# Scaling the top-k threshold on GpSimd in the main loop of an attention-and-FFN kernel, with a reordered tail

## The chip, the cores and the metric

The kernel runs on one core of a Trainium2 chip. The metric is the device time of one execution in microseconds (us). A core has a matmul engine (TensorE, PE in the profile; its weight loads are PEld), VectorE (DVE), ScalarE (ACT), GpSimd (POOL) and SyncE (SP, which here only starts DMAs). Each engine takes its instructions in the order in which the program wrote them and waits on semaphores for data of the others.

## The reference

Attention over 8 batches, 8 heads, 576 rows and a head size of 64, of which each row keeps only its 32 largest scores, and then a feed-forward layer with a squared ReLU:

```python
scores = scale * np.matmul(q, k.transpose(0, 1, 3, 2))
kth = np.partition(scores, -top_k, axis=-1)[..., -top_k:-top_k + 1]     # top_k = 32
mask = scores >= kth
scores = np.where(mask, scores, -1000000000.0)
scores = scores - np.max(scores, axis=-1, keepdims=True)
attn = np.exp(scores)
attn = attn / (np.sum(attn, axis=-1, keepdims=True) + 1e-09)
x = np.matmul(attn, v)                 # heads side by side: 4608 rows x 512
h = np.maximum(x @ w_in, 0.0)          # 512 x 2048
out = h * h @ w_out                    # 2048 x 512
```

## The kernel before

The rows of scores are worked off in 144 steps (U = 144). A step u holds two tiles of 128 rows by 576 scores. Lines 658 to 709 are the main loop over steps 0 to 124 (Z = U - 19 = 125); lines 721 to 762 are steps 125 to 141, and two steps and an ending are written out behind them. All work is issued in an order written out by hand: `pin` keeps every instruction at its place on its engine, so the order of the calls in a step is the order on each engine's queue.

What a step does for its two tiles:

- `scores(u + 2)` (L195): PE computes the scores of the step after next into the two halves sc_a and sc_b, and ACT copies each half to SBUF (L210), the two score copies of a step.
- `split(u + 1)` (L224): DVE folds the 576 scores of a row with maxima and minima into `cat` (L235, L236, L243, L244, and L242 where the far minimum is DVE's own). `small_mins(u + 1)` (L254) makes the remaining minima on POOL as an integer addition and subtraction (L258, L259). Where the planner has lent the far minimum to POOL, `far_copy(u + 1)` (L249) lets ACT copy the far maxima from PSUM (L252).
- `topk(u)` (L267): DVE finds the 32 largest in four rounds of eight (MAX8 at L277, MATCH_REPLACE8 at L281). In round 1 `negate` (L313) takes, in every second step and for two steps at once, the negated maximum on DVE (L318), and ACT adds a constant to it (`low`, L320), which is the bias of the exponentials.
- `cut(u - 1)` (L324): one small instruction on ACT multiplies the 32nd largest score of the step before by a huge negative constant (`edge`, L326). `below(u - 1, x)` (L328) is the mark: ACT computes a ReLU of scores times that constant plus `edge` into `kept` (L330), for each of the two tiles. `expo(u - 1, x)` (L336) is the exponential of a tile into `w_two` (L338). `mask(u - 1)` (L332) adds `kept` to `w_two` as integers on POOL (L334), and `turn(u - 1)` (L369) starts a DMA transpose on SP's queue into `wT`.
- `products(u - 3)` (L648): PE multiplies `wT` with the values (L399); column 64 is the sum of weights. `invert` or `invert_two` (L402, L407) is its reciprocal on DVE (L404, L411), and `place` (L420) scales and stores the output of a tile on ACT (L428, L436).
- The feed-forward layer is cut into pieces of some 1 to 2 us of matmuls, which `dense` and `piece` (L563, L554) put between the attention's matmuls. What an up piece leaves for ACT (a ReLU, L511) and POOL (the square, L514) is queued in `late` and issued by the next `flush`; so is the copy of a finished output (L538).
- `prepare` (L622) transposes and scales inputs of later heads (L135 to L149 on ACT, L155 on POOL, the values), with loads on SP's queue; 16 weight casts go to ACT or POOL (L600, L597). `verify` and `note` check now and then, on DVE and POOL (L303 to L311), that the shortcut of the top-k was exact.

`owe` and `pass_step` are a planner's account: each step books 4.6 us for ACT and 3.2 us for POOL besides what single jobs book, and 6.1 us are written off for each step; `split` lends to POOL, and a cast chooses its engine, by these accounts.

In the main loop a step's calls stand in this order: cut(u - 1) and the first mark; split(u + 1); place; far_copy(u + 1); second mark; round 0; checks; small_mins(u + 1); a dense piece; scores(u + 2); rounds 1 to 3; exponentials, mask and transpose of u - 1; flush; products(u - 3); a second dense piece; preparation. In the tail (`for u in range(Z, U - 2)`) the exponentials, mask and transpose of step u - 1 are issued in `weights(u - 1)`: for even u after small_mins, for odd u after round 3, since the constant of two steps is made together.

Of the kernel before, what the change touches and what calls it, by code (L numbers as in the profile page):

```python
# [13 lines left out]
f32 = mybir.dt.float32  # L14
# [3 lines left out]
ALU = mybir.AluOpType  # L18
AF = mybir.ActivationFunctionType
# [4 lines left out]
def kernel(  # L24
# [9 lines left out]
    nc = tc.nc  # L34
# [5 lines left out]
    scale = 1.0 / (D ** 0.5)  # L40
    STEEP = 2.0 ** 80
    PREV = 1.0 - 2.0 ** -24
    LOW, SPAN, FINE = -76.24618986, 11.0, 2.0 ** -60
# [3 lines left out]
    def pin(ins):  # L47
        tc.keep_in_program_order(ins)
        return ins
# [3 lines left out]
    def owe(**more):  # L53
        for e, t in more.items():
            debt[e] += t
# [10 lines left out]
    small = fast.enter_context(tc.tile_pool(name="small", bufs=2))  # L66
# [4 lines left out]
    fill = const.tile([128, 512], bf16, name="fill")  # L71
# [100 lines left out]
    for b in range(B):  # L172
# [8 lines left out]
        for c in range(4):  # L181
            steps += [((i, c, 0), (i, c, 1)) for i in range(p0 + 1, p0 + 4)]
            if c == 0:
                steps += rests(p0 + 2)
    U = len(steps)
    first = {}
    for u, two in enumerate(steps):
        for i, c, a in two:
# [3 lines left out]
    st = {}  # L192
# [31 lines left out]
    def split(u, meanwhile=None):  # L224
        d = st[u]
        lend = 2 < u < U - 20 and debt["G"] < 4.9 and debt["A"] < 5.4
        if lend:
# [35 lines left out]
    held_m = {}  # L263
# [3 lines left out]
    def topk(u, rounds=(0, 1, 2, 3), between=None):  # L267
        d = st[u]
        g = u % GROUP
        if g == 0 and 0 in rounds:  # L270
            held_m["m"] = small.tile([128, GROUP, 2, 4, 8], f32, name="m", bufs=2)
        m = d["m"] = [held_m["m"][:, g, :, r, :] for r in range(4)]
        cat = d["cat"]
        for r in rounds:
            at = WINDOWS[r]
            for x in range(2):
                pin(nc.vector.max(out=m[r][:, x, :], in_=cat[:, x, at]))  # L277
            if r == 3:
                break
            for x in range(2):  # L280
                pin(nc.vector.match_replace(out=cat[:, x, at], in_to_replace=m[r][:, x, :], in_values=cat[:, x, at], imm_value=NEG))  # L281
            if r == 1:
                negate(u)
            if r == 2 and between:
                between()
        if g == GROUP - 1 and 3 in rounds and u < U - 1:
            verify(u)
# [23 lines left out]
            pin(nc.gpsimd.tensor_tensor(odd, odd, wide[:, n], op=ALU.add))  # L311

    def negate(u):  # L313
        if u % 2 == 0:
            return
        g = u % GROUP
        neg = small.tile([128, 2, 2, 1], f32, name="neg", bufs=3)
        pin(nc.vector.tensor_reduce(neg[:, :, :, :], held_m["m"][:, g - 1:g + 1, :, 0:2, 0], axis=mybir.AxisListType.X, op=ALU.max, negate=True))  # L318
        low = small.tile([128, 2, 2, 1], f32, name="low", bufs=3)
        pin(nc.scalar.activation(low[:, :, :, :], neg[:, :, :, :], AF.Copy, bias=LOW))  # L320
        for n in range(2):
            st[u - 1 + n].update(neg=neg[:, n], low=low[:, n])

    def cut(u):  # L324
        edge = st[u]["edge"] = small.tile([128, 2, 1], f32, name="edge", bufs=3)
        pin(nc.scalar.activation(edge[:, :, :], st[u]["m"][3][:, :, 7:8], AF.Copy, scale=-STEEP * PREV))  # L326

    def below(u, x):  # L328
        d = st[u]
        pin(nc.scalar.activation(kept[u % 2][:, x, :].bitcast(f8)[:, 1:2 * S:2], d["s"][:, x, :], AF.Relu, bias=d["edge"][:, x, :], scale=STEEP, saturate=False))  # L330
# [5 lines left out]
    def expo(u, x):  # L336
        d = st[u]
        pin(nc.scalar.activation(w_two[u % 3][:, x, 0:S], d["s"][:, x, :], AF.Exp, bias=d["low"][:, x, :]))  # L338
# [6 lines left out]
    late, squares = [], []  # L345
    hold = {"squares": False, "out": False}

    def square():
        while squares:
            squares.pop(0)(nc.gpsimd)  # L350
# [7 lines left out]
    def expo_last(x):  # L358
        d = st[U - 1]
        e = kept[(U - 1) % 2][:, x, :].bitcast(bf16)  # L360
        pin(nc.scalar.activation(e, d["s"][:, x, :], AF.Exp, bias=d["neg"][:, x, :]))
        last_e.append(e)

    def mask_last(x):
        d = st[U - 1]
        pin(nc.vector.scalar_tensor_tensor(out=w_two[(U - 1) % 3][:, x, 0:S], in0=d["s"][:, x, :], scalar=d["m"][3][:, x, 7:8],
                                           in1=last_e[x], op0=ALU.is_ge, op1=ALU.mult))
# [80 lines left out]
    def x_unit(now, b, c):  # L448
# [21 lines left out]
        else:  # L470
            pin(nc.sync.dma_start_transpose(out=to, in_=x_tok[b, c][:, :]))
            ripe.setdefault(now + (3 if now < Z - 8 else 2), []).append(done)

    def rem_unit(now, b):
# [8 lines left out]
        if b % 2:  # L483
            rem = xt_rem[g % 2]
            stores = [[(slice(64 * a, 64 * a + 64), out[(b - 1 + a) * S + 512:(b + a) * S]) for a in range(2)]]
            go = lambda: block(lambda kh: rem[:, kh, :], stores)
            if now < Z - 1:
                ripe.setdefault(now + 1, []).append(go)
# [117 lines left out]
    load_pair(0)  # L606
    load_pair(1)
    busy = ps_one.tile([128, 512], f32, name="dn_ps")
    for n in range(11):
        pin(nc.tensor.matmul(out=busy[:, :], lhsT=fill[:, 0:128], rhs=fill[:, :], start=(n == 0), stop=(n == 10)))  # L610
    soon, coming = prep_units(0), 1
    for _ in range(4):
        soon.pop(0)()
# [26 lines left out]
    scores(1)  # L640


    Z = U - 19

    def ok(w):
        return 0 <= w < U

    def products(w):  # L648
        if ok(w):
            for x in range(2):  # L650
                weigh(w, x)
# [5 lines left out]

    for u in range(Z):
        f = u - 4
        pass_step()  # L660
        owe(A=4.6, G=3.2)
        if u > 0:
            cut(u - 1)
            below(u - 1, 0)
        if u == 0:
            topk(0, (0, 1))
            split(1)
            topk(0, (2, 3))
        else:
            split(u + 1, (lambda: invert_two(f)) if ok(f) and f % 2 else None)  # L670
        if ok(f - 1):
            place(f - 1)
        far_copy(u + 1)
        if u > 0:
            below(u - 1, 1)
            topk(u, (0,))
        if checks:
            note()
        small_mins(u + 1)
        dense(u, 0)  # L680
        for i, c, a in steps[u + 2]:
            while coming <= i or (coming == i + 1 and soon):
                prepare(u)
        scores(u + 2)
        if u > 0:
            topk(u, (1, 2, 3))
            exps(u - 1)
            mask(u - 1)
            turn(u - 1)
        flush()  # L690
        products(u - 3)
        if u == Z - 1:
            assert u % 2 == 0
            products(u - 2)
            invert_two(u - 3)
            place(u - 4)
            place(u - 3)
        else:
            dense(u, 1)
            flush()  # L700
        for _ in range(2 if u < 8 or u in (U - 22, U - 19) else 1):
            prepare(u)
        if 1 < u < 24 and not ups and not downs:
            idle_piece(2)
        turn_x(u)
        if w_casts and u >= 3:
            w_casts.pop(0)()
        if w_loads and u >= 1:
            w_loads.pop(0)()

    def weights(w):
        expo(w, 0)
        expo(w, 1)
        mask(w)
        turn(w)

    def move():
        while moves:
            moves.pop(0)(u)

    for u in range(Z, U - 2):
        cut(u - 1)
        below(u - 1, 0)
        move()
        below(u - 1, 1)
        split(u + 1)
        topk(u, (0,))
        if u == Z:
            invert(u - 3)
            place(u - 3)  # L730
        if checks:
            note()
        small_mins(u + 1)
        if squares:
            squares.pop(0)(nc.gpsimd)
        if u % 2 == 0:
            weights(u - 1)
        square()
        hold["squares"] = False
        for go in ripe.pop(u, ()):  # L740
            go()
        for i, c, a in steps[u + 2]:
            while coming <= i or (coming == i + 1 and soon):
                prepare(u)
        scores(u + 2)
        topk(u, (1,))
        products(u - 2)
        if not piece():
            idle_piece()
        topk(u, (2,), lambda: invert(u - 2))  # L750
        topk(u, (3,))
        if u % 2:
            weights(u - 1)
        flush()
        place(u - 2)
        turn_x(u)
        hold["squares"] = True
        for n in range(3 if u >= U - 12 else 2):
            if not piece() and n == 0:
                idle_piece()  # L760
        for _ in range(2 if u == U - 19 else 1):
            prepare(u)
# [3 lines left out]
    u = U - 2  # L766
# [13 lines left out]
    products(u - 2)  # L780
    topk(u, (2,), lambda: invert(u - 2))
    topk(u, (3,))
    late.pop()()
    square()
    ups.pop(0)()
    flush()
    square()
# [33 lines left out]
    u = U - 1  # L821
    cut(u - 1)
    below(u - 1, 0)
    below(u - 1, 1)
    topk(u, (0, 1))
    weights(u - 1)
    expo_last(0)
    late.pop(0)()
    expo_last(1)
    late.pop(0)()  # L830
    products(u - 2)
    downs.pop(0)()
    downs.pop(0)()
# [43 lines left out]
    for z in range(4):  # L877
        for j in range(2):
            for f in range(4 * z, 4 * z + 4):
                pin(nc.tensor.matmul(out=halves[j][:, 0:256], lhsT=hl[:, f, 0:128], rhs=w_out[:, f, 256 * j:256 * j + 256],  # L880
                                     start=(f == 0), stop=(f == NF - 1)))
# [132 lines left out]
```

## Time and profile before

The median of 3 runs is 954.59 us (953.52 to 955.2).

| What | before |
|---|---|
| profiled execution | 955.07 us |
| its span, first to last instruction | 953.3 us |
| mean granted TensorE clock | 0.914 |
| instructions | 18831 |
| steps 1 to 124 (19.25 to 789.50 us) | 770.25 us |
| tail and ending (789.50 to 953.30 us) | 163.80 us |

A row of a group gives line, engine, operation, what is written and read with shapes, the count, and behind the bar busy time and mean duration (ns), then the engine's idle time in front of the group and what ended it. A row in order of time gives start, duration, engine, line, operation, and in square brackets the idle time in front of it with its releaser. A row of a wait gives who waited for whom, the sum, the number of times and the longest. A row of a stretch gives the stretch, its length, the busy time of PE, PEld, DVE, ACT and POOL in us with their counts, the granted clock, the DMA share and GB/s.

### The profile page before, as it was taken

How to read it: one execution, taken by the hardware profiler on the slowest of the kernel's cores; microseconds unless marked ns; L12 is line 12 of the kernel's file. 1: busy time of each engine (PE TensorE's matmuls, PEld its weight loads, DVE VectorE, ACT ScalarE, POOL GpSimd, SP SyncE). 2: the span in 40 equal slices, each digit the busy share in tenths (PEclk: the TensorE clock that was granted, in tenths of full speed). 3: DMA queues.
4: the chain of work that ended last, by engine and by line, in shares of the span. 5: the costliest groups of instructions: out<-in, count | busy, mean ns of one | idle time of the engine just before them, and what ended most of it. 6: DMA issues, size and time to landing. Idle time of an engine off the chain costs nothing.

```text
span 953.3 us, 18831 instructions
## 1 busy us (share of the span) xinstructions
PE 769.7 (81%) x5343; PEld 447.7 (47%) x5343; DVE 900.5 (94%) x3674; ACT 845.3 (89%) x1860; POOL 788.8 (83%) x731
## 2 busy tenths in 40 slices
PE   7798878888887877877877888888888788788877
PEld 3444334445444434544544444444544444545545
DVE  6999989999999999999999999999999998898885
ACT  4879979999999999999989999999999997879674
POOL 5889888998899988988998878998889894867562
PEclk9989988998899999899988889888999997989999
DMA  5677765344544555344554355544545545232231
GB/s 111 152 182 165 178 126 105 85 103 89 124 96 93 108 120 110 67 91 104 109 116 104 69 91 124 106 93 97 106 102 113 110 84 105 59 67 65 65 75 44
DMA packets 326880, 98.00 MB, mean 103 GB/s; under 512 B 318960, under 2 KB 319216, under 8 KB 326768
## 3 DMA queue, kind: packets, MB, share of 16 engines
q1 hardware_dynamic: 325424, 96.28, 48.4%
q8 instruction: 45, 0.74, 0.3%
q14 instruction: 67, 0.55, 0.2%
q10 hardware_dynamic: 1344, 0.43, 0.2%
HBM read 36.70 MB, written 9.44 MB: 48 GB/s over the span
## 4 chain that ended last, share of the span: by engine, by line
DVE 40%; ACT 23%; PE 16%; POOL 9%; DMA 5%; issue 5%; SPq 1%; ACTq 0%; POOLq 0%; DVEq 0%
DVE m L277 19%; DVE cat L281 9%; ACT s L210 4%; PE gen L505 3%; PE dn_ps L528 3%; ACT kept_a L330 3%; DVE cat L243 3%; DVE sc_b L235 3%; PE av_ps L399 3%; DVE tops L236 3%; ACT kept_b L330 3%; DVE cat L244 2%; POOL cat L258 2%; ACT rl L511 2%; PE sc_b L206 2%
## 5 line engine op out<-in xcount | busy, mean ns | idle before, releaser
L277 DVE MAX8 m<-cat 128x8 f32<-128x104 f32 (+3 forms) x1152 | 439.4, 423 | 0.0
L281 DVE MATCH_REPLACE8 cat<-m,cat 128x104 f32<-128x104 f32 (+2 forms) x864 | 261.9, 311 | 0.0
L258 POOL TENSOR_TENSOR cat<-s 128x576 int32<-128x576 int32 (+1 forms) x144 | 177.2, 1231 | 16.0 <-DVE m L277 9.6
L259 POOL TENSOR_TENSOR cat<-cat,tops 128x576 int32<-128x576 int32 (+1 forms) x144 | 177.0, 1229 | 12.1 <-ACT tops L252 0.8
L514 POOL TENSOR_TENSOR h<-rl 128x512 bf16<-128x512 f32 x138 | 143.6, 1041 | 32.2 <-ACT rl L511 31.6
L528 PE MATMUL dn_ps<-w_out,h 128*128 128x512 bf16 x560 | 162.6, 422 | 5.6 <-ACT wide L538 4.8
L206 PE MATMUL sc_b<-qkT 64*128 64x288 f32 x512 | 98.4, 462 | 73.2 <-ACT tops L252 68.2
L505 PE MATMUL gen<-xT,w_in 128*128 128x256 bf16 (+1 forms) x1088 | 149.1, 291 | 9.0 <-ACT rl L511 7.4
L399 PEld LDWEIGHTS <-wT 128*128 128x128 bf16 (+3 forms) x1600 | 93.2, 102 | 119.1 <-issue 43.3
L505 PEld LDWEIGHTS <-w_in 128*128 128x128 bf16 x1344 | 121.9, 108 | 42.0 <-issue 18.7
L206 PE MATMUL sc_a<-qkT 64*128 64x288 f32 x512 | 103.6, 480 | 25.7 <-DVE tops L236 10.5
L330 ACT ACTIVATE kept_a<-s,edge 128x576 fp8e3<-128x576 f32 x144 | 110.7, 776 | 6.9
L330 ACT ACTIVATE kept_b<-s,edge 128x576 fp8e3<-128x576 f32 x142 | 109.8, 777 | 6.3
L210 ACT ACTIVATE s<-sc_a 128x576 f32<-128x576 f32 x144 | 93.1, 647 | 11.3 <-PE sc_a L206 8.5
L206 PEld LDWEIGHTS sc_b<-qkT 64*128 64x128 f32 x512 | 45.3, 198 | 119.5 <-ACT tops L252 105.5
L210 ACT ACTIVATE s<-sc_b 128x576 f32<-128x576 f32 x144 | 94.1, 654 | 7.7 <-PE sc_b L206 6.2
L511 ACT ACTIVATE rl<-gen 128x512 f32<-128x512 f32 x140 | 83.2, 594 | 19.9 <-PE gen L505 19.6
L528 PEld LDWEIGHTS <-h 128*128 128x128 bf16 x560 | 53.3, 105 | 58.4 <-issue 23.6
L235 DVE TENSOR_TENSOR sc_b<-sc_a,s 128x288 f32<-128x288 f32 x144 | 64.9, 451 | 14.3 <-ACT s L210 14.2
L206 PEld LDWEIGHTS sc_a<-qkT 64*128 64x128 f32 x512 | 43.0, 198 | 72.5 <-ACT edge L326 30.0
L338 ACT ACTIVATE w_two_a<-s,low 128x576 bf16<-128x576 f32 x96 | 71.7, 778 | 0.7
L338 ACT ACTIVATE w_two_b<-s,low 128x576 bf16<-128x576 f32 x96 | 71.4, 774 | 0.7
(168 smaller groups left out, 1390.7 us busy)
## 6 DMA issues: line engine op xcount, KB each, us to landing
q_raw<-in_q_dram SPq DMA_DIRECT2D x64, 128.0 KB, 3.0
v_raw<-in_v_dram SPq DMA_DIRECT2D x64, 128.0 KB, 3.0
k_raw<-in_k_dram SPq DMA_DIRECT2D x62, 128.0 KB, 2.9
out_dram<-wide SPq DMA_DIRECT2D x31, 256.0 KB, 2.7
wide<-in_moe_w_in_dram SPq DMA_DIRECT2D x8, 512.0 KB, 5.3
wide<-in_moe_w_out_dram SPq DMA_DIRECT2D x8, 512.0 KB, 4.5
out_dram<-wide SPq DMA_DIRECT2D x9, 128.0 KB, 2.5
q_raw<-in_q_dram SPq DMA_DIRECT2D x32, 32.0 KB, 2.5
```

The costliest lines, as they stand in the source:

```text
L206: pin(nc.tensor.matmul(out=ps[j][:, x, 0:HALF], lhsT=lhsT, rhs=rhs, start=True, stop=True))
L210: pin(nc.scalar.activation(s[:, :, j * HALF:(j + 1) * HALF], ps[j][:, :, 0:HALF], AF.Copy))
L258: pin(nc.gpsimd.tensor_tensor(at, s[:, :, 0:n].bitcast(i32), s[:, :, HALF:HALF + n].bitcast(i32), op=ALU.add))
L259: pin(nc.gpsimd.tensor_tensor(at, at, d["tops"][:, :, 0:n].bitcast(i32), op=ALU.subtract))
L277: pin(nc.vector.max(out=m[r][:, x, :], in_=cat[:, x, at]))
L281: pin(nc.vector.match_replace(out=cat[:, x, at], in_to_replace=m[r][:, x, :], in_values=cat[:, x, at], imm_value=NEG))
L330: pin(nc.scalar.activation(kept[u % 2][:, x, :].bitcast(f8)[:, 1:2 * S:2], d["s"][:, x, :], AF.Relu, bias=d["edge"][:, x, :], scale=STEEP, ...
L338: pin(nc.scalar.activation(w_two[u % 3][:, x, 0:S], d["s"][:, x, :], AF.Exp, bias=d["low"][:, x, :]))
L399: pin(nc.tensor.matmul(out=o[rows], lhsT=wT[0:kc, 5 * x + n, rows], rhs=va[0:kc, n, h, :], start=(n == 0), stop=(n == 4)))
L505: pin(nc.tensor.matmul(out=hp[:, n * n_rows:(n + 1) * n_rows], lhsT=w_in[:, kh, (f0 + n) * 128:(f0 + n + 1) * 128], rhs=xt(kh), start=(kh ...
L514: squares.append(lambda by: pin(by.tensor_mul(h2, flat, flat)))
L528: pin(nc.tensor.matmul(out=op[:, :], lhsT=held["h2"][:, f, c * 128:(c + 1) * 128], rhs=w_out[:, f, :], start=(f == 0), stop=(f == NF - 1)))
```

## The change

In the main loop the threshold's scaling (`cut`) goes from ACT to POOL for the thresholds of steps 0 to 123, where it is the first call of the step. The calls on ACT are put in another order: placing and the far copy come first, then the first mark; the second mark moves behind the score copies. The planner books 0.2 us less for ACT and 0.2 us more for POOL in each step.

In the tail every step takes its own negated maximum (from step 124 on; the last step has no `low`), the exponentials of a step are issued at the end of that same step, a step sooner than before, and mask and transpose of the step before follow the two marks after split, round 0 and small_mins. In the last step they follow the marks at once. One of eleven fill matmuls at the start is left out.

```diff
     U = len(steps)
+    Z = U - 19
...
     def negate(u):
-        if u % 2 == 0:
+        n = 2 if u < Z - 1 else 1
+        if u % 2 == 0 and n == 2:
             return
         g = u % GROUP
-        neg = small.tile([128, 2, 2, 1], f32, name="neg", bufs=3)
-        pin(nc.vector.tensor_reduce(neg[:, :, :, :], held_m["m"][:, g - 1:g + 1, :, 0:2, 0], axis=mybir.AxisListType.X, op=ALU.max, negate=True))
-        low = small.tile([128, 2, 2, 1], f32, name="low", bufs=3)
-        pin(nc.scalar.activation(low[:, :, :, :], neg[:, :, :, :], AF.Copy, bias=LOW))
-        for n in range(2):
-            st[u - 1 + n].update(neg=neg[:, n], low=low[:, n])
+        neg = small.tile([128, 2, 2, 1], f32, name="neg", bufs=3)[:, 0:n]
+        pin(nc.vector.tensor_reduce(neg, held_m["m"][:, g + 1 - n:g + 1, :, 0:2, 0], axis=mybir.AxisListType.X, op=ALU.max, negate=True))
+        low = small.tile([128, 2, 2, 1], f32, name="low", bufs=3)[:, 0:n]
+        if u < U - 1:
+            pin(nc.scalar.activation(low, neg, AF.Copy, bias=LOW))
+        for z in range(n):
+            st[u + 1 - n + z].update(neg=neg[:, z], low=low[:, z])
 
     def cut(u):
         edge = st[u]["edge"] = small.tile([128, 2, 1], f32, name="edge", bufs=3)
-        pin(nc.scalar.activation(edge[:, :, :], st[u]["m"][3][:, :, 7:8], AF.Copy, scale=-STEEP * PREV))
+        t = st[u]["m"][3][:, :, 7:8]
+        if u < Z - 1:
+            pin(nc.gpsimd.tensor_scalar(edge[:, :, :], t, scalar1=-STEEP * PREV, scalar2=None, op0=ALU.mult))
+        else:
+            pin(nc.scalar.activation(edge[:, :, :], t, AF.Copy, scale=-STEEP * PREV))
...
-    for n in range(11):
-        pin(nc.tensor.matmul(out=busy[:, :], lhsT=fill[:, 0:128], rhs=fill[:, :], start=(n == 0), stop=(n == 10)))
+    for n in range(10):
+        pin(nc.tensor.matmul(out=busy[:, :], lhsT=fill[:, 0:128], rhs=fill[:, :], start=(n == 0), stop=(n == 9)))
...
     for u in range(Z):
         f = u - 4
         pass_step()
-        owe(A=4.6, G=3.2)
+        owe(A=4.4, G=3.4)
         if u > 0:
             cut(u - 1)
-            below(u - 1, 0)
...
         far_copy(u + 1)
         if u > 0:
-            below(u - 1, 1)
+            below(u - 1, 0)
             topk(u, (0,))
...
         scores(u + 2)
         if u > 0:
+            below(u - 1, 1)
             topk(u, (1, 2, 3))
             exps(u - 1)
             mask(u - 1)
...
         if u == Z - 1:
             assert u % 2 == 0
+            expo(u, 0)
+            expo(u, 1)
             products(u - 2)
...
     def weights(w):
-        expo(w, 0)
-        expo(w, 1)
         mask(w)
         turn(w)
...
     for u in range(Z, U - 2):
         cut(u - 1)
         below(u - 1, 0)
+        below(u - 1, 1)
         move()
-        below(u - 1, 1)
         split(u + 1)
         topk(u, (0,))
...
         small_mins(u + 1)
-        if squares:
-            squares.pop(0)(nc.gpsimd)
-        if u % 2 == 0:
-            weights(u - 1)
+        weights(u - 1)
         square()
...
         topk(u, (3,))
-        if u % 2:
-            weights(u - 1)
+        expo(u, 0)
+        expo(u, 1)
         flush()
         place(u - 2)
...
     topk(u, (3,))
+    expo(u, 0)
     late.pop()()
     square()
+    expo(u, 1)
     ups.pop(0)()
...
     below(u - 1, 1)
+    weights(u - 1)
+    late.pop(0)()
     topk(u, (0, 1))
-    weights(u - 1)
     expo_last(0)
     late.pop(0)()
     expo_last(1)
-    late.pop(0)()
```

More of the change, by code (lines that the diff above doesn't have):

```diff
@@ L640 @@
     scores(1)
-    Z = U - 19
     def ok(w):
```

## The prediction

> **What bounds the kernel now.** I read the busy times first, then the same by stage, then who waits for whom, then the order of time of one step. The first line is from the page, the two others are the stretches of the main loop (from the first threshold scaling, step 1, to that of step 124: 123 periods) and of the tail.
>
> ```profile
> PE 769.7 (81%) x5343; PEld 447.7 (47%) x5343; DVE 900.5 (94%) x3674; ACT 845.3 (89%) x1860; POOL 788.8 (83%) x731
> ```
> ```profile
> 19.25:789.50 770.25, 625.67 (x4216) 355.70 (x4215) 755.22 (x3102) 717.08 (x1589) 681.01 (x594) 0.91 0.53 110
> 789.50:953.30 163.80, 130.20 (x1064) 84.88 (x1063) 135.40 (x541) 121.05 (x260) 96.24 (x102) 0.90 0.31 67
> ```
>
> In the main loop a step takes 770.25/123 = 6.26 us, and VectorE (DVE) works for 755.22 of 770.25 (98%), ScalarE (ACT) for 717 (93%), GpSimd (POOL) for 681 (88%). In the tail DVE is idle for 28.4 of 163.8 us. What DVE waited for in the main loop:
>
> ```profile
> DVE sc_b L235 <- ACT s L210: 11.0, 15, 1.4
> DVE rsums L411 <- PE av_ps L399: 2.1, 2, 1.5
> ```
>
> So the loop is DVE's, with ACT close behind, and nobody shows a wait of DVE or ACT for POOL. That freedom is what to watch: POOL may run late by a microsecond or two, and nobody on ACT notices. One whole step of ACT in order of time, and POOL beside it:
>
> ```profile
> 368.83 0.78 ACT L330 ACTIVATE kept_a<-s,edge 128x576 fp8e3<-128x576 f32 x1
> 369.51 0.50 ACT L428 ACTIVATE x_tok<-av_ps,rsums 128x64 bf16<-128x64 f32 x2
> 370.00 0.41 ACT L252 ACTIVATE tops<-sc_b 128x288 f32<-128x288 f32 x1
> 370.31 0.77 ACT L330 ACTIVATE kept_a<-s,edge 128x576 fp8e3<-128x576 f32 x1
> 370.98 0.64 ACT L210 ACTIVATE s<-sc_a 128x576 f32<-128x576 f32 x1
> 371.51 0.65 ACT L210 ACTIVATE s<-sc_b 128x576 f32<-128x576 f32 x1
> 372.04 0.21 ACT L320 ACTIVATE low<-neg 128x4 f32<-128x4 f32 x1
> 372.29 1.44 ACT L338 ACTIVATE w_two_c<-s,low 128x576 bf16<-128x576 f32 x2
> 373.63 0.57 ACT L511 ACTIVATE rl<-gen 128x512 f32<-128x512 f32 x1
> ...
> 374.68 0.20 ACT L326 ACTIVATE edge<-m 128x2 f32<-128x2 f32 x1
> 374.97 0.78 ACT L330 ACTIVATE kept_b<-s,edge 128x576 fp8e3<-128x576 f32 x1
> ```
> ```profile
> 373.80 1.40 POOL L334 TENSOR_TENSOR w_two_c<-w_two_c,kept_a 128x576 int32<-128x576 int32 x1 [0.80 <-ACT w_two_c L338]
> 375.17 1.04 POOL L514 TENSOR_TENSOR h<-rl 128x512 bf16<-128x512 f32 x1
> 376.16 1.40 POOL L258 TENSOR_TENSOR cat<-s 128x576 int32<-128x576 int32 x1
> ```
>
> The reader is to see three things. Spacing, start to start, is shorter than the duration (0.68 for a mark of 0.78), so I count spacings. POOL's mask (L334) starts 0.07 after the second exponential ends (373.73). And POOL is free for the next step's first instruction (L258) only at 376.16, while ACT began that step with its threshold (L326) at 374.68, 1.48 us sooner.
>
> **The change, main loop.** The threshold's scaling leaves ACT and becomes the first instruction of POOL's step. POOL takes its work in the written order: the mask and, behind it, the squares and the value scaling of the step before stand ahead of it. Behind the scaling wait, on ACT, the first mark, the two score copies, the second mark and the two exponentials; and the mask that POOL does next waits for these. So the change closes a ring of one turn per step: scaling (POOL), marks, copies and exponentials (ACT), mask, square (POOL), next scaling. Its length, from the rows above:
>
> - ACT: first mark 0.68 (368.83 to 369.51), copies 0.53 and 0.53, second mark 0.67, exponentials 1.44: 3.85. Output placing and far copy drop out, since they now stand ahead of the first mark.
> - hand-over to POOL 0.07; mask 1.37 (373.80 to 375.17); hand-over back to ACT, which no row shows, taken as 0.07 too.
> - the scaling itself on POOL: no row shows it. Bounds below.
>
> How much else falls into the ring, and whether the step shown is typical, from the groups of the main loop (first ACT, then POOL; the last row is from the whole run):
>
> ```profile
> L330 ACT ACTIVATE kept_a<-s,edge 128x576 fp8e3<-128x576 f32 x124 | 96.2, 777 | 6.1
> L210 ACT ACTIVATE s<-sc_b 128x576 f32<-128x576 f32 x123 | 80.6, 656 | 5.1 <-PE sc_b L206 3.7
> L338 ACT ACTIVATE w_two_a<-s,low 128x576 bf16<-128x576 f32 x82 | 61.7, 779 | 0.7
> L511 ACT ACTIVATE rl<-gen 128x512 f32<-128x512 f32 x108 | 64.1, 593 | 8.3 <-PE gen L505 8.0
> L326 ACT ACTIVATE edge<-m 128x2 f32<-128x2 f32 x123 | 25.5, 207 | 4.6 <-DVE m L277 4.5
> L320 ACT ACTIVATE low<-neg 128x4 f32<-128x4 f32 x62 | 13.4, 215 | 0.0
> L538 ACT ACTIVATE wide<-dn_ps 128x512 f32<-128x512 f32 x26 | 15.6, 599 | 0.0
> ```
> ```profile
> L514 POOL TENSOR_TENSOR h<-rl 128x512 bf16<-128x512 f32 x108 | 112.5, 1041 | 19.0 <-ACT rl L511 18.6 <-DMA v_raw<-in_v_dram 0.4
> L334 POOL TENSOR_TENSOR w_two_c<-w_two_c,kept_a 128x576 int32<-128x576 int32 x21 | 29.5, 1406 | 11.5 <-ACT w_two_c L338 11.5
> L155 POOL TENSOR_SCALAR vau_b<-v_raw 128x512 bf16<-128x512 f32 (+1 forms) x10 | 10.1, 1011 | 0.8
> L597 POOL CAST w_in<-wide 128x1024 bf16<-128x1024 f32 x8 | 8.3, 1038 | 0.8 <-DMA wide<-in_moe_w_in_dram 0.7
> L597 POOL CAST w_out<-wide 128x1024 bf16<-128x1024 f32 x7 | 7.3, 1038 | 4.1 <-DMA wide<-in_moe_w_out_dram 2.0 <-ACT kept_b L330 2.0
> L305 POOL TENSOR_SCALAR size<-m 128x48 f32<-128x48 f32 x5 | 1.9, 375 | 0.3
> L309 POOL TENSOR_SCALAR wide_off<-wide_off 128x96 f32<-128x96 f32 x5 | 2.2, 448 | 0.4
> L634 POOL MEMSET ones<- 128x1 f32 x1 | 0.1, 99 | 0.1
> ```
>
> The scaling is a GpSimd tensor_scalar on 2 elements a partition. The rows L305 and L309 (same operation, 48 and 96 elements: 375 and 448 ns) make 1.5 ns an element and 302 ns at 2: I take 0.30. The smallest POOL row, 0.10, is the lower end, 0.45 the upper. What ACT sheds (L326, 25.5 us in all) gains nothing by itself if ACT waits in the ring.
>
> The plain ring is 3.85 + 0.07 + 1.37 + 0.30 + 0.07 = 5.66, times 123 = 696. Into it come:
> - 108 relu-and-square pairs. Behind the mask, as at 375.17, the square puts 0.99 into the ring; between the two exponentials the relu puts 0.48 on ACT and the square ends some 0.33 after the second exponential, 0.81. I take 0.93: 100.
> - values: L155 has six such rows, one for each vau buffer, two instructions of 1.01 for each of 29 pairs, between mask and scaling: 59.
> - 62 lower bounds (L320) at 0.25 (372.04 to 372.29): 15.
> - weight casts on POOL, 8 of w_in and 7 of w_out at 1.04: 16 if all stay, 0 if the new cost entries (ACT 0.2 less, POOL 0.2 more) send them to ACT. I take 8.
> - 26 copies of finished output, of which I take two thirds to fall between the exponentials, 0.48 each: 8.
> - five times the checks, which stand between scaling and L258:
>
> ```profile
> 316.80 0.30 POOL L303 TENSOR_TENSOR flags<-m,least 128x48 bf16<-128x48 f32 x1
> 320.18 1.41 POOL L258 TENSOR_TENSOR cat<-s 128x576 int32<-128x576 int32 x1
> 323.02 1.42 POOL L334 TENSOR_TENSOR w_two_c<-w_two_c,kept_b 128x576 int32<-128x576 int32 x1
> ```
>
> There POOL needs 6.22 from scaling to mask where ACT needs about 4: 2.2 each, 11.
>
> Sum: 696 + 100 + 59 + 15 + 8 + 8 + 11 = 897 us for 123 steps, 7.3 a step, against 770: **+127**. What covers itself: DVE's 6.14 a step (755.22/123) lies beside the ring, so far copies that the new entries turn back into a minimum on DVE cost nothing while DVE has over a microsecond to spare in a step; without that cover each would lengthen DVE's step. The far copy ahead of the mark lets PE's second score matmul start sooner, which hides behind ACT's wait. The wT transposes on SP's queue go out with the later mask; their products stand two steps further on and wait no longer than now. The one fill matmul less at the start is counted as nothing, as the first load decides there. Bounds of the stage: scaling 0.10 or 0.45 (-25, +18), casts (-8, +8), hand-over back 0 or 0.2 (-9, +16), score matmuls that come late for the copies, 0 to 0.2 a step (+25): +85 to +194, the ends not all together.
>
> **The change, tail.** From step 125 on each step takes its own maximum and does the exponentials at the end of the step before, so that mask and transpose follow the marks at once. What they are late for now:
>
> ```profile
> DVE rsum L404 <- PE av_ps L399: 14.6, 10, 2.1
> POOL w_two_c L334 <- ACT w_two_c L338: 16.3, 7, 5.5
> L318 DVE TENSOR_REDUCE neg<-m 128x4 f32<-128x8 f32 x10 | 1.6, 155 | 0.0
> ```
>
> DVE waits 14.6 us in its reciprocal for the products of the transposed weights; the masks wait up to 5.5 us for exponentials. Most of DVE's wait should go. Against it stand about ten more maxima on DVE (10 x 0.155 = 1.6) and ACT's exponentials (1.44) ahead of output placing and the next threshold, which is late next. I take -10; ends -18 (the wait and a part of the other idle time) and +5 (an exponential pair ahead of every other threshold, half of it seen, in seven steps). The other edits of the tail (a relu's place at the end, a square that is no longer drawn ahead) move single instructions of the same kind within a step and count as nothing.
>
> **Sum.** The profiled execution took 955.07 (span 953.3), the median of the runs is 954.59; a difference below 0.2% (1.9 us) is no difference here. 955 + 127 - 10 = 1072; against the median 1071.
>
> **The rivals.**
> 1. No ring, and ACT's relief counts: faster. Mechanism: POOL reaches the scaling before ACT has finished what stands between exponentials and first mark (from 373.63 to 374.68 and then placing and far copy, 0.80: in all 1.8 us). It decides where mask, square and scaling together stay under 1.8. For it: DVE's only large wait, 11.0, is for ACT's copies, and ACT sheds 25.5. Against it: mask and square alone are 2.36. Time: 955 - 13 - 10 = 932.
> 2. Nothing but busy time counts. DVE stays the fullest engine and POOL rises by 124 x 0.30 to 718 of 770, still under it; so the loop stays at 770 and the tail's gain is given back to its extra work: 955. The Trainium skill, Perfetto Trace Analysis, section Identifying the Most-Contended Engine, says to judge Vector, Scalar and GpSimd by occupancy and to work on the fullest first; by that rule DVE's 98% decides and the loop does not move. The trace here agrees on who is fullest, but holds no case of POOL standing in ACT's way.
> 3. The ring closes, but without the squares: if these are late enough to stand behind the next scaling, 897 - 100 = 797, and 955 + 27 - 10 = 972. For it: POOL waited 18.6 us for relus. Against: the square at 375.17 follows the mask with no gap, ahead of L258. The Trainium skill, the same page, section Tensor Engine Instruction, calls ACT, DVE and GPSIMD strict FIFO; the trace agrees, L514 of one step ahead of L258 of the next, and by that the squares stay in the ring.
>
> **How the numbers follow.** The ring with squares 0.82 (own range 1030 to 1115), rival 3 0.05, rival 1 0.09, rival 2 0.04. Slower 0.87, faster 0.09, same 0.04. The ring's range holds about 0.76; down to rival 3's 970 the range holds 0.81.
>
> **What would show it.** In the changed profile: ACT's first mark waits for POOL's edge in most steps, about a microsecond each and over 100 us in all; POOL waits for ACT's exponentials in nearly every step (about 1.2 us); DVE's wait for s (L210) grows from 11 to over 100 and its share falls below 88% in the loop; the scaling takes 0.3; the main loop takes near 900 us. In the tail the wait of the reciprocal falls below 5 and mask follows the second mark. The prediction is wrong if ACT's marks start without waiting for POOL, or if DVE keeps its 98%.

## The result and the profile after

The changed kernel takes 1080.6 us (median of 4 runs, 1079.74 to 1081.98), the kernel before 954.62 beside it: ratio 1.132, 95% interval 1.130 to 1.134. The profiled execution took 1079.89 us, its span is 1078.1. Forecast were 1071 us and a range of 970 to 1115.

The busy times of the changed kernel, and then its stretches with the same columns as before, the main loop from the first threshold scaling to that of step 124, and the rest:

```profile
PE 805.8 (75%) x5268; PEld 472.1 (44%) x5342; DVE 907.8 (84%) x3677; ACT 831.2 (77%) x1756; POOL 819.7 (76%) x851
```
```profile
18.20:928.70 910.50, 671.77 (x4178) 385.61 (x4235) 768.69 (x3119) 703.84 (x1480) 715.63 (x717) 0.84 0.46 94
928.70:1078.10 149.40, 120.65 (x1037) 79.86 (x1048) 130.01 (x528) 120.85 (x265) 93.31 (x100) 0.92 0.32 69
```

The loop is 140 us longer (910.5 against 770.25) and the tail 14 us shorter (149.4 against 163.8). No engine is full any more: VectorE did 755 us of work in a loop of 770 and does 769 in a loop of 910. Who waits for whom, in the main loop of the changed kernel (lines have moved: the mark is L337, the GpSimd scaling L331, a score copy L211, the exponential L345, the mask L341, the square L521):

```profile
DVE sc_b L236 <- ACT s L211: 139.3, 111, 4.6
ACT kept_a L337 <- POOL edge L331: 129.0, 54, 5.9
POOL h L521 <- ACT rl L518: 57.1, 40, 3.7
ACT kept_b L337 <- POOL edge L331: 53.8, 57, 2.2
POOL w_two_b L341 <- ACT w_two_b L345: 42.3, 27, 3.5
POOL w_two_a L341 <- ACT w_two_a L345: 40.2, 26, 3.8
POOL w_two_c L341 <- ACT w_two_c L345: 35.9, 25, 2.9
```

ScalarE's marks wait 183 us for GpSimd's scaling (in 111 of the 123 steps), GpSimd's masks 118 us for ScalarE's exponentials (in 78), and VectorE, which waited 11 us for score copies, now waits 139. Two engines that wait for each other in nearly every step are what the prediction called the ring. One plain turn of it in order of time, first GpSimd, then ScalarE:

```profile
399.91 0.22 POOL L331 TENSOR_SCALAR edge<-m 128x2 f32<-128x2 f32 x1
...
404.33 1.40 POOL L341 TENSOR_TENSOR w_two_b<-w_two_b,kept_a 128x576 int32<-128x576 int32 x1 [1.34 <-ACT w_two_b L345]
405.69 0.22 POOL L331 TENSOR_SCALAR edge<-m 128x2 f32<-128x2 f32 x1
```
```profile
400.16 0.78 ACT L337 ACTIVATE kept_a<-s,edge 128x576 fp8e3<-128x576 f32 x1 [0.40 <-POOL edge L331]
400.85 0.63 ACT L211 ACTIVATE s<-sc_a 128x576 f32<-128x576 f32 x1
401.38 0.64 ACT L211 ACTIVATE s<-sc_b 128x576 f32<-128x576 f32 x1
401.91 0.78 ACT L337 ACTIVATE kept_a<-s,edge 128x576 fp8e3<-128x576 f32 x1
402.57 0.20 ACT L323 ACTIVATE low<-neg 128x4 f32<-128x4 f32 x1
402.81 1.44 ACT L345 ACTIVATE w_two_b<-s,low 128x576 bf16<-128x576 f32 x2
...
405.95 0.78 ACT L337 ACTIVATE kept_b<-s,edge 128x576 fp8e3<-128x576 f32 x1 [0.41 <-POOL edge L331]
```

From scaling to scaling it is 5.78 us (399.91 to 405.69), with a lower bound of 0.24 in it and no square. Counted over the trace, turns in which GpSimd does the two minima, the mask and nothing else take 5.75 on average (5 turns); with one square behind the mask 6.82 (42 turns); with the values of a pair behind it 8.15 (9 turns). Of the 108 squares, 67 stand behind the mask, between it and the next scaling; the other 41 stand between the minima and the mask.

### The profile page after: what moved, and what is told of

The parts are those of the page before. It is cut to its first block, busy times and chain, and to the rows that moved or that the text cites. A ratio compares the mean times of both kernels' runs of the same rounds, so it can differ in the third digit from the quotient of the medians.

```text
span 1078.1 us, 18769 instructions
## 1 busy us (share of the span) xinstructions
PE 805.8 (75%) x5268; PEld 472.1 (44%) x5342; DVE 907.8 (84%) x3677; ACT 831.2 (77%) x1756; POOL 819.7 (76%) x851
## 4 chain that ended last, share of the span: by engine, by line
ACT 27%; POOL 27%; DVE 19%; issue 13%; PE 8%; DMA 2%; SPq 2%; POOLq 0%; ACTq 0%; DVEq 0%
ACT s L211 9%; DVE m L278 7%; POOL h L521 5%; DVE cat L282 4%; POOL cat L259 3%; ACT w_two_a L345 3%; POOL w_two_c L341 3%; ACT w_two_c L345 3%; ACT w_two_b L345 3%; POOL cat L260 3%; ACT kept_a L337 3%; POOL w_two_b L341 2%; POOL w_two_a L341 2%; PE sc_b L207 2%; ACT kept_b L337 2%
## 5 line engine op out<-in xcount | busy, mean ns | idle before, releaser
L337 ACT ACTIVATE kept_a<-s,edge 128x576 fp8e3<-128x576 f32 x144 | 110.7, 776 | 130.2 <-POOL edge L331 129.0
L259 POOL TENSOR_TENSOR cat<-s 128x576 int32<-128x576 int32 (+1 forms) x144 | 181.2, 1258 | 17.7 <-DVE m L278 10.0
L521 POOL TENSOR_TENSOR h<-rl 128x512 bf16<-128x512 f32 x138 | 143.3, 1042 | 62.2 <-ACT rl L518 61.9
L260 POOL TENSOR_TENSOR cat<-cat,tops 128x576 int32<-128x576 int32 (+1 forms) x144 | 181.2, 1258 | 11.3
L512 PE MATMUL gen<-xT,w_in 128*128 128x256 bf16 (+1 forms) x1088 | 157.0, 300 | 43.7 <-ACT rl L518 42.6
L535 PE MATMUL dn_ps<-w_out,h 128*128 128x512 bf16 x498 | 147.5, 417 | 36.6 <-ACT wide L545 27.1
L207 PE MATMUL sc_b<-qkT 64*128 64x288 f32 x512 | 107.3, 500 | 78.2 <-ACT tops L253 72.2
L512 PEld LDWEIGHTS <-w_in 128*128 128x128 bf16 x1344 | 124.8, 110 | 91.6 <-issue 63.3
L337 ACT ACTIVATE kept_b<-s,edge 128x576 fp8e3<-128x576 f32 x142 | 109.2, 775 | 57.6 <-POOL edge L331 56.9
L406 PEld LDWEIGHTS <-wT 128*128 128x128 bf16 (+3 forms) x1600 | 96.4, 105 | 99.2 <-issue 58.7
L207 PE MATMUL sc_a<-qkT 64*128 64x288 f32 x512 | 110.5, 510 | 14.4 <-DVE tops L237 8.8
L207 PEld LDWEIGHTS sc_b<-qkT 64*128 64x128 f32 x512 | 50.7, 218 | 122.7 <-ACT tops L253 105.5
L211 ACT ACTIVATE s<-sc_a 128x576 f32<-128x576 f32 x144 | 91.4, 635 | 11.8 <-PE sc_a L207 8.7
L211 ACT ACTIVATE s<-sc_b 128x576 f32<-128x576 f32 x144 | 92.6, 643 | 7.9 <-PE sc_b L207 7.5
L345 ACT ACTIVATE w_two_a<-s,low 128x576 bf16<-128x576 f32 x96 | 71.1, 770 | 0.8
L345 ACT ACTIVATE w_two_b<-s,low 128x576 bf16<-128x576 f32 x96 | 71.1, 768 | 0.7
```

Of the source, the lines that this page charges most:

```text
L207: pin(nc.tensor.matmul(out=ps[j][:, x, 0:HALF], lhsT=lhsT, rhs=rhs, start=True, stop=True))
L211: pin(nc.scalar.activation(s[:, :, j * HALF:(j + 1) * HALF], ps[j][:, :, 0:HALF], AF.Copy))
L259: pin(nc.gpsimd.tensor_tensor(at, s[:, :, 0:n].bitcast(i32), s[:, :, HALF:HALF + n].bitcast(i32), op=ALU.add))
L260: pin(nc.gpsimd.tensor_tensor(at, at, d["tops"][:, :, 0:n].bitcast(i32), op=ALU.subtract))
L406: pin(nc.tensor.matmul(out=o[rows], lhsT=wT[0:kc, 5 * x + n, rows], rhs=va[0:kc, n, h, :], start=(n == 0), stop=(n == 4)))
L512: pin(nc.tensor.matmul(out=hp[:, n * n_rows:(n + 1) * n_rows], lhsT=w_in[:, kh, (f0 + n) * 128:(f0 + n + 1) * 128], rhs=xt(kh), start=(kh ...
```

## The experiments

The theory is the ring. Rival A: the new order of ScalarE's work is to blame. Rival B: the time or load that the scaling puts on GpSimd is, wherever it stands. Loop lengths below are taken from the first mark to the first mark of step 124 (770 before, 910 in the changed kernel).

**e1: the scaling back on ScalarE, all else as changed.**

```diff
-        if u < Z - 1:
-            pin(nc.gpsimd.tensor_scalar(edge[:, :, :], t, scalar1=-STEEP * PREV, scalar2=None, op0=ALU.mult))
-        else:
-            pin(nc.scalar.activation(edge[:, :, :], t, AF.Copy, scale=-STEEP * PREV))
+        pin(nc.scalar.activation(edge[:, :, :], t, AF.Copy, scale=-STEEP * PREV))
```

> The changed kernel with the scaling back on ScalarE and all else as changed (order of marks and far copy, planner entries, tail). Theory, the ring: without GpSimd between two steps of ScalarE the loop falls back to VectorE's work, 755 to 775 us for 123 steps, and the tail stays at 149: 930 to 950 us in all. Rival A, the new order on ScalarE is to blame: it stays over 1050. Rival B, only GpSimd's time for 124 scalings counts (27 us busy): about 1054.

Measured: 931.5 us, ratio to the kernel before 0.974 (0.969 to 0.980). The wait of VectorE for copies in this kernel, and its loop:

```profile
DVE sc_b L236 <- ACT s L211: 6.5, 9, 2.4
```
```profile
19.30:781.00 761.70, 604.62 (x4157) 349.55 (x4217) 753.47 (x3100) 709.59 (x1602) 685.11 (x590) 0.93 0.55 112
```

149 us of the changed kernel's time hang on which engine scales the threshold. Rival A falls: with the new order the loop is even shorter than before. Rival B's 1054 falls too.

**e2: the scaling stays on GpSimd, but ahead of the mask of the step before.**

```diff
         owe(A=4.4, G=3.4)
-        if u > 0:
-            cut(u - 1)
         if u == 0:
             topk(0, (0, 1))
             split(1)
             topk(0, (2, 3))
+            cut(0)
...
             topk(u, (1, 2, 3))
+            if u < Z - 1:
+                cut(u)
             exps(u - 1)
             mask(u - 1)
```

> The changed kernel with the scaling still on GpSimd, but written right behind the fourth round of its own step, ahead of the mask of the step before. Theory, the ring: the scaling no longer stands behind mask and square, so the ring is open; loop 755 to 785, total 930 to 960, and ScalarE's wait for edge falls from 186 us to under 30. Rival B, a slow or contended GpSimd instruction, or GpSimd's load: still above 1050.

Measured: 945.4 us, ratio 0.989 (0.982 to 0.995); loop 776.7. The same 124 instructions on the same engine, in another place of its queue, cost nothing like 140 us. The waits for the scaling in this kernel:

```profile
ACT kept_a L337 <- POOL edge L331: 13.1, 8, 2.9
POOL edge L331 <- DVE m L278: 12.0, 8, 4.6
ACT kept_b L337 <- POOL edge L331: 9.0, 13, 1.0
```

ScalarE waits 22 us instead of 186 (whole run), and GpSimd's queue now waits 12 us for VectorE's fourth round, which it did only once in the changed kernel (1.1 us). That it stays 14 us behind e1 fits these two waits; it was not taken apart further. Rival B falls in its form "load".

**e4: the kernel before with the scaling alone moved to GpSimd.**

```diff
-        pin(nc.scalar.activation(edge[:, :, :], st[u]["m"][3][:, :, 7:8], AF.Copy, scale=-STEEP * PREV))
+        t = st[u]["m"][3][:, :, 7:8]
+        if u < U - 20:
+            pin(nc.gpsimd.tensor_scalar(edge[:, :, :], t, scalar1=-STEEP * PREV, scalar2=None, op0=ALU.mult))
+        else:
+            pin(nc.scalar.activation(edge[:, :, :], t, AF.Copy, scale=-STEEP * PREV))
```

> The kernel before with only the scaling moved to GpSimd for thresholds 0 to 123; marks, far copy and tail as before. Theory, the ring: placing and far copy (0.80 a step) now lie inside the ring too, 98 us more than in the changed kernel's loop of 910, and the tail of before (164): 1150 to 1195. Rival A, the new order is to blame: near 955 to 985. Rival B, only the instruction's own time: 955 to 982.

Measured (one run): 1200.2 us, 5 above the expected range; loop 1013.5, expected 1008.

```profile
ACT kept_a L334 <- POOL edge L328: 177.8, 60, 6.0
```

Putting placing and the far copy ahead of the mark takes them out of the ring: 1013.5 - 909.9 = 104 us, or 0.84 a step, against 0.80 read from the spacing of the rows 369.51 to 370.31 of the kernel before. Some 4 us of it are not theirs: with the planner entries of before, 15 weight casts of about 1 us run on GpSimd here, and 11 in the changed kernel. The order of ScalarE's work softens the ring; it doesn't cause it.

**e6 and e7: two memsets on GpSimd, just ahead of the scaling, or just behind it.** They write a tile that nobody reads.

```diff
+            for _ in range(2):
+                pin(nc.gpsimd.memset(idle[:, :], 0.0))       # 128x320 bf16; e6
             cut(u - 1)
+            for _ in range(2):
+                pin(nc.gpsimd.memset(idle[:, :], 0.0))       # the same; e7
```

> The changed kernel with two memsets of 128x320 (bf16, estimated 0.3 to 0.37 us each from the rows of 128x256 and 128x512) on GpSimd just ahead of the scaling, in steps 1 to 124. They compute nothing that is used. Theory, the ring: they lengthen every turn by their full time, 75 to 90 us: 1150 to 1170. If GpSimd's position in the ring does not matter, only its load: less than 30 us, 1080 to 1110.

> The same two memsets just behind the scaling, ahead of the minima. Theory, the ring: GpSimd waits 0.9 us a step for the exponentials there, so most of it is hidden: 1080 to 1105. If it is the load of GpSimd that costs: the same as with the filler ahead of the scaling.

Measured (one run each): 1159.1 us ahead, 1081.1 behind, where the changed kernel takes 1080.6. The group in e6, and the loops of e6 and e7 (the fifth busy time is GpSimd's):

```profile
L670 POOL MEMSET idle<- 128x320 bf16 x248 | 90.3, 364 | 8.3
```
```profile
19.00:1008.80 989.80, 705.86 (x4179) 399.09 (x4236) 768.03 (x3117) 700.93 (x1480) 797.25 (x963) 0.80 0.42 87
```
```profile
20.50:932.10 911.60, 666.72 (x4169) 383.88 (x4226) 766.62 (x3115) 702.43 (x1479) 796.16 (x961) 0.84 0.46 94
```

GpSimd is busy for 797 and 796 us, the same, against 716 in the changed kernel. Ahead of the scaling the filler lengthens the loop by 80 us, nearly its whole busy time; behind it, by 2. This pair shows the ring most directly: what stands between mask and scaling is paid nearly in full, what stands between scaling and mask lies beside ScalarE's turn.

**e3: squares held back until behind the next scaling, unless a down piece or a third square in line draws them sooner.**

```diff
         if u > 0:
             cut(u - 1)
+        square()
+        hold["squares"] = True
...
+                    if len(squares) == 2 and in_loop[0]:
+                        square()
                     squares.append(lambda by: pin(by.tensor_mul(h2, flat, flat)))
...
         def down(c, part):
             def go():
+                if in_loop[0]:
+                    square()
```

> The changed kernel with the squares of a step held back until the next step's scaling is issued (unless a down piece needs them sooner). Theory, the ring with squares in it: 108 squares of 0.99 and the growth of their wait for relus (from 19 to 57 us) leave the ring, 107 to 145 us less, so 936 to 975. If the squares were not in the ring (rival 3 of the prediction): within 20 us of 1080.

Measured: 1051.5 us, ratio 1.101 (1.093 to 1.109); loop 880.8. A miss: 29 us came off where 107 to 145 were expected. The waits of the two marks in this kernel:

```profile
ACT kept_a L337 <- POOL edge L331: 112.2, 44, 6.6
ACT kept_b L337 <- POOL edge L331: 41.7, 35, 3.1
```

They fell only from 112 waits to 79 (of 124) and from 186 to 154 us. The traces show that the edit does not empty the ring of squares: 34 squares still stand between mask and next scaling, where 67 did. In 29 steps it even puts one there that stood ahead of the mask in the changed kernel, since a down piece behind the mask, or a third square in line, now draws the one that was held. One such step on GpSimd, in the changed kernel and then in e3:

```profile
198.10 1.04 POOL L521 TENSOR_TENSOR h<-rl 128x512 bf16<-128x512 f32 x1 [1.16 <-ACT rl L518]
199.10 1.41 POOL L341 TENSOR_TENSOR w_two_a<-w_two_a,kept_a 128x576 int32<-128x576 int32 x1
200.47 0.22 POOL L331 TENSOR_SCALAR edge<-m 128x2 f32<-128x2 f32 x1
```
```profile
196.43 1.40 POOL L341 TENSOR_TENSOR w_two_a<-w_two_a,kept_a 128x576 int32<-128x576 int32 x1 [1.82 <-ACT w_two_a L345]
197.80 1.03 POOL L523 TENSOR_TENSOR h<-rl 128x512 bf16<-128x512 f32 x1
198.80 0.21 POOL L331 TENSOR_SCALAR edge<-m 128x2 f32<-128x2 f32 x1
```

Step by step, from scaling to scaling: the 62 turns that lost the square behind their mask became 47 us shorter (0.75 each), the 29 turns that got one there 17 us longer (0.60 each), the other 32 turns 2.6 us longer, 27 less in all (29 from mark to mark). So squares do lengthen the ring, but this run is no test of a ring without them. The expectation was wrong besides: it took all 108 squares at 0.99 and the whole growth of GpSimd's wait for relus. But all 40 of these waits in the changed kernel's loop (57.1 us) stand in front of squares ahead of the mask, where GpSimd has to wait for the exponentials anyway, and the relu's own 0.48 stays in the ring when its square goes.

**e8: the value scaling held back as well.**

```diff
         if soon:
-            soon.pop(0)()
+            go = soon.pop(0)
+            if in_loop[0] and go.__name__ == "values":
+                held_values.append(go)
+            else:
+                go()
...
         square()
         hold["squares"] = True
+        while held_values:
+            held_values.pop(0)()
```

> The kernel with the squares held back until behind the scaling (1051), with the value scaling held back in the same way. Theory: 29 steps with values took 8.6 to 9.2 us there against 6.6 for the others; about 2.1 us leave each, so 975 to 1000. If the values were long only because they fall on steps that are long anyway: over 1035.

Measured: 1011.2 us, ratio 1.057 (1.049 to 1.066); loop 844.9. It is 36 us less than e3, where 51 to 76 were expected: a miss. The squares stand as in e3, 34 of them still behind the mask. Step by step against e3, the 29 turns that had values behind the mask became 63 us shorter, 2.2 each, as expected; but the 28 turns that now have them between scaling and mask became 30 us longer. One of these turns on GpSimd:

```profile
416.53 0.21 POOL L331 TENSOR_SCALAR edge<-m 128x2 f32<-128x2 f32 x1
416.72 1.03 POOL L523 TENSOR_TENSOR h<-rl 128x512 bf16<-128x512 f32 x1
417.83 2.10 POOL L155 TENSOR_SCALAR vau_d<-v_raw 128x512 bf16<-128x512 f32 x2
420.00 1.41 POOL L259 TENSOR_TENSOR cat<-s 128x576 int32<-128x576 int32 x1
421.48 1.41 POOL L260 TENSOR_TENSOR cat<-cat,tops 128x576 int32<-128x576 int32 x1
422.85 1.40 POOL L341 TENSOR_TENSOR w_two_b<-w_two_b,kept_a 128x576 int32<-128x576 int32 x1
424.22 0.22 POOL L331 TENSOR_SCALAR edge<-m 128x2 f32<-128x2 f32 x1
```

There is no gap: GpSimd's own work in this step is 7.69 us (416.53 to 424.22), and in 26 of the 28 turns GpSimd is idle for 0.32 us at most. The long step is now GpSimd's own, and after each of the 28 ScalarE's next mark waits for the scaling, 40 us in all. In the kernel before, GpSimd ran 1.48 us behind ScalarE (376.16 against 374.68) without holding it up; that this slack would even out long steps, and is lost in the ring, is argued from these rows, and no run isolates it.

**e5: the main loop of before with the changed tail.** In the main loop the scaling is on ScalarE, the first mark stands ahead of split, the second behind the far copy, and the planner books 4.6 and 3.2, as before.

```diff
-        owe(A=4.4, G=3.4)
+        owe(A=4.6, G=3.2)
         if u > 0:
             cut(u - 1)
+            below(u - 1, 0)
...
         if u > 0:
-            below(u - 1, 0)
+            below(u - 1, 1)
             topk(u, (0,))
...
         if u > 0:
-            below(u - 1, 1)
             topk(u, (1, 2, 3))
```

> The main loop of the kernel before (scaling on ScalarE, marks ahead, planner entries of before) with the changed tail. Theory: the tail is 14 us shorter by itself (149.4 in the changed kernel, 163.8 before), so 937 to 945. If the tail's gain came only because the slower loop hands over a rested pipeline: 950 to 957. The distance to the changed kernel with the scaling back on ScalarE (931) is what the new order of marks and far copy is worth: about 9.

Measured: 938.6 us, ratio 0.982 (0.976 to 0.988). The tail's gain is its own: from first mark to first mark of step 124 the loop takes 770.2 us, as before, and the rest 147.8 against 163.5; the reciprocal's wait for products in the tail (14.6 us before) is no longer among VectorE's waits in this kernel.

**e11 and e12: e1 and e5 again, side by side on one chip.** The edits are those of e1 and e5.

> The same kernel as the changed one with the scaling back on ScalarE, beside the tail alone on the same chip, since their distance (931.5 and 938.6) was taken on two chips. If the new order of marks and far copy with its planner entries is worth something: 0.972 to 0.978 of the kernel before, and 5 to 9 us under the tail alone. If not: within 3 us of it.

> The tail alone, beside the kernel above: 0.980 to 0.985 of the kernel before, 14 to 19 us less than it. If the order is worth nothing the two kernels lie within 3 us.

Measured: 927.4 us, ratio 0.973 (0.969 to 0.976), against 937.8 us, ratio 0.984 (0.979 to 0.988). The new order with its planner entries, 7 more far copies (109 against 102) and 4 weight casts fewer on GpSimd is worth 10 us once the scaling is on ScalarE. Which of these it is was not tested.

**e9 and e10: e1 with more far minima lent to GpSimd.**

```diff
-        owe(A=4.4, G=3.4)
+        owe(A=4.4, G=3.0)      # e9; e10: owe(A=4.0, G=2.6)
```

> The changed kernel with the scaling on ScalarE and GpSimd's planner entry lowered from 3.4 to 3.0, so that more far minima are lent to GpSimd (109 lent in the run before, 16 kept in steps that could lend). With VectorE busy for 753 of 761 us of the loop, each further loan saves 0.44 us there and adds about 1.2 on GpSimd. If VectorE alone sets the loop: some 8 more loans, 3 to 4 us less than 931.5, so 925 to 931. If GpSimd (685 of 761) is already near its limit: no gain, 930 to 940.

> The same with entries of 4.0 for ScalarE and 2.6 for GpSimd, so that nearly every far minimum is lent (about 120). VectorE alone: 5 to 7 us less than 931.5, 923 to 930. If GpSimd's late minima then hold back the fourth round, or ScalarE's copies the step: 932 to 950.

Measured: 932.4 us, ratio 0.976 (0.973 to 0.978), and 934.7 us, ratio 0.977 (0.975 to 0.980), with 115 and 120 far copies. The loop of e10:

```profile
19.90:785.00 765.10, 613.21 (x4217) 347.57 (x4217) 750.77 (x3090) 709.73 (x1610) 701.09 (x593) 0.93 0.54 111
```

VectorE did less work (750.8 against 753.5 in e1), and the loop was not shorter (765.1 against 761.7). The lower entries also sent 4 and 3 more weight casts to GpSimd; what holds the loop there was not taken apart. No kernel that ran is clear of e1 on the fast side, and e1 beats both kernels, the one before and the changed one.

## Why the prediction was right, and where it was off

- **The ring** was the mechanism, and its place was as predicted. Forecast for the loop was +127, measured +140. e1 and e2 open it in two ways and both come out below the kernel before (e2 by its tail alone, with a loop of 776.7 against 770); e6 and e7 show that place, not load, decides.
- **The size: part of the closeness is luck.** The loop was some 13 us longer than the 897 of the sum, but that is a difference of larger errors. The scaling with its hand-over back was put too high: 0.37 in the sum, 0.26 in the trace (405.69 to 405.95), so 123 x 0.11 = 14 us too much. Drawing the line through 48 and 96 elements on down to 2 was the error. Against it stand some 27 us too little, 12 of them a term that the sum took at nothing and only the bounds had: in the ring, ScalarE's score copies waited 12.1 us for TensorE's score matmuls.

```profile
ACT s L211 <- PE sc_a L207: 6.9, 10, 1.3
ACT s L211 <- PE sc_b L207: 5.2, 15, 0.9
```

A pair of values is another 8: from mask to scaling a turn with one takes 3.69 below (410.35 to 414.04; 3.68 on average), against 1.37 on average with a mask alone. That is 2.3 where the sum had 2.02, 29 times. Weight casts (11 on GpSimd, where 8 us were taken) and the spacing of the score copies (0.54 where 0.53 was taken) make about 3 each.

```profile
410.35 1.40 POOL L341 TENSOR_TENSOR w_two_c<-w_two_c,kept_b 128x576 int32<-128x576 int32 x1 [1.58 <-ACT w_two_c L345]
411.84 2.12 POOL L155 TENSOR_SCALAR vau_c<-v_raw 128x512 bf16<-128x512 f32 x2
414.04 0.22 POOL L331 TENSOR_SCALAR edge<-m 128x2 f32<-128x2 f32 x1
```

- **Squares and relus** were sized rightly in all. The 67 squares behind the mask put 1.0 each into the ring (mask to scaling takes 2.37 on average where one square follows, 1.37 where none does); the other 41 come with a relu between the exponentials, 0.48 on ScalarE, and end some 0.33 after the exponential. That makes 67 + 33 = 100 us, the sum's figure.
- **Sum of terms against maxima.** The sum took each turn as the ring's length. In the changed kernel that holds nearly always (112 of 124 first marks wait for the scaling). Where terms are taken out of the ring it holds less: in e3 45 of the 124 marks no longer wait, and in e8 26 turns are full of GpSimd's own work. So terms of the ring do not come off one by one as they add up.
- **The tail**: forecast -10, measured -14. The reciprocal's wait fell from 14.6 to 3.3 us:

```profile
DVE rsum L411 <- PE av_ps L406: 3.3, 2, 3.1
```

- **Rival 1**, ScalarE's relief: not seen in this kernel; moving the scaling off ScalarE in an open ring (e2) ended 14 us above leaving it there (e1). **Rival 2**, occupancy decides: wrong here. The loop moved by 140 us, and its fullest engine is busy for 768.69 of 910.50 (84%). The rule of the Trainium skill named there (Perfetto Trace Analysis, section Identifying the Most-Contended Engine: optimize the engine of highest occupancy first) points to VectorE. The trace agrees that it stayed the fullest, but it waited 139 us for score copies that the ring held up. **Rival 3**, squares behind the scaling: in the changed kernel none of the 108 stands between the scaling and the minima, and 67 stand between mask and scaling, as the prediction said. What the ring would take without them was not measured, as e3 moved only a part.
- **What would show it**: ScalarE's wait for the scaling was forecast at over 100 us (183 in the loop), VectorE's for copies at over 100 (139) and its share below 88% (84%), the loop near 900 (910), the reciprocal's wait below 5 (3.3). The scaling's 0.3 was off (0.219), and GpSimd's wait for exponentials in nearly every step came in 78 of 123 (1.5 each); in 40 others GpSimd waits for a relu, in front of a square.

## What to carry to other kernels

Before moving a small instruction to an engine with time to spare, follow what it waits behind on that engine's queue and who waits for it: if the thing ahead of it waits for the engine that waits for it, two engines that ran a step apart are tied together, and the turn of the ring, not anybody's busy time, can set the step. A filler put just ahead of and just behind the suspect tells such a ring from load (e6 and e7). Often another place in the same queue opens it (e2), and the cheapest place may still be the engine it came from (e1).

## What the runs showed that was not expected

- A GpSimd scaling of 2 elements a partition takes 0.219 us, less than the straight line through those of 48 and 96 elements gave (0.302).
- The granted TensorE clock went with the time: 0.914 before, 0.851 in the changed kernel, 0.814 in e4, 0.93 in e1. In the kernels that are held up by the ring TensorE is less busy (75% in the changed kernel and 70% in e4, against 81% before and 80% in e1) and its clock is lower; whether the lower clock adds to the ring was not tested.
